# One order between pairs widened: xh and xl ahead of the next sine and of the next pair's planes, in every pair from batch 1 on

## The chip, the cores and the metric

The kernel runs on one core of one Trainium2 chip. The metric is the device time of one execution in microseconds, the median of several runs.

## What is computed

The reference is an attention over 8 batches of 8 heads (512 local rows with a window of 32 to each side, and 32 global rows that see all and are seen by all), followed by a layer with a cosine on all 8 x 544 rows. Cut to what matters:

```python
k_all = concat([k_g, k_l]); v_all = concat([v_g, v_l])
out_g = sm(scale * q_g @ k_all.T) @ v_all                       # 32 rows
s_ll  = where(abs(i - j) <= 32, scale * q_l @ k_l.T, -1e9)      # 512 rows
out_l = sm(concat([scale * q_l @ k_g.T, s_ll])) @ v_all
x = concat([out_g, out_l]) -> rows of 8 heads x 64 = 512
h = x @ w_in                # 512 -> 2048
out = (h * cos(h)) @ w_out  # 2048 -> 512
```

## The kernel before

**Attention** goes by batch b (0 to 7) and pair of heads p (0 to 3). For each of four windows i of 128 rows, TensorE makes the scores (`sc_a`, L527), VectorE adds the mask and takes the row minimum mn (`sc_b`, L545), ScalarE takes the exponential (`sc_c`, through `table_act`, L425), and VectorE the reciprocal of the sums (L564 and L565). Then `sc_d` makes two fp16 planes of the probabilities, the high one on ScalarE (L592) and what it misses on VectorE (L593): eight instructions a pair on each engine, all in the four buffers named planes. SP's queue transposes them (`sc_e`, L612) into pt, and TensorE multiplies pt by the values' two parts vh and vl into the PSUM tile acc (`av_a`, L645). `av_b` takes acc out of PSUM, again as two parts: **xh** on ScalarE (L665) and **xl** on VectorE (L666). xl is the last to read acc. The global rows have a path of their own, from gps (L681) to planes_g and gacc.

**Values.** The next batch's values are loaded into vr (`load_v`, one buffer, 1.25 MB), VectorE takes their maximum vm in one instruction (L481), TensorE spreads it over the partitions into pm_v (L459), VectorE makes the scale of it (L491), and `v_d` makes vh on ScalarE (L511) and vl on VectorE (L512), a pair at a time. The load of the next batch has to wait for the last vl.

**The layer** goes by chunks c of 256 rows, two to a batch (c = 2b and 2b + 1, which follow in the next batch's time), with eight steps j each, and one chunk at the end for the global rows. A step is 24 matmuls with xh and xl into the PSUM tile ph (L800); u on ScalarE (L822) and VectorE (L823), which brings h to its period; the sine w on ScalarE (`m1_c`, L425); its square on GpSimd (L838); gf on VectorE (L840); gh on ScalarE (L844); gl on GpSimd (L845); and, three steps later, 12 matmuls into po (L859 to L861). VectorE and ScalarE scale po into the output rows o.

**PSUM** has a pool of three buffers with the tag att, which ps, gps, acc, gacc and pm_v take in turn, three for ph and two for po.

**What sets the order.** Each piece of work is put at a slot and a phase by `at(slot, phase, ...)`; there are eight slots to a chunk. In batches 2 to 7 pair p of batch b has its time t = 16(b - 1) + 3 + 4p: scores at t - 7 and t - 5, exponentials at t - 4, planes at t - 3, transposes at t - 1, product, xh and xl at t. So the planes of the next pair (t + 4 - 3) come one slot behind xh and xl. From this listing a scheduler with a model of the engines' times makes each engine's final order, and it may let one instruction pass another where nothing forbids it. What forbids it are dependences on data and edges of the kind `order`, which the kernel adds with `tc.add_manual_dep`; such an edge fixes the order of two instructions of one engine, and puts no semaphore into the program. `table_act` has one that keeps exponentials and sines in the order in which they are written. A sine and an exponential use different function tables on ScalarE, so each change between them is an ACT_TABLE_LOAD (58 in the program).

Two such edges concern xh and xl. `av_b` keeps the two instructions of the batch's latest pair in `st["last_x", b]`. Where p is 0 and b over 1, `sc_d` puts the planes of the pair behind xh and xl of the batch before (that is, of its pair 3). And `m1_c` puts the sine of an odd chunk's last step behind xh of the pair 3 that stands there.

Of the kernel before, what the change touches and what calls it, by code (L numbers as in the profile page):

```python
# [57 lines left out]
NS = NJ // 2  # L58
# [60 lines left out]
def body(tc, qf, v, wi, wo, mask, out):  # L119
# [5 lines left out]
    with ExitStack() as ctx:  # L125
# [37 lines left out]
        def behind(ins, what, why="scale_first"):  # L163
            if st.get(what) is not None:
                tc.add_manual_dep(ins, st[what].name, order, reason=why)
# [253 lines left out]
        st = {}  # L419
        order = mybir.DependencyInfo(mybir.DependencyClass.NoSync, mybir.DependencyReason.DATA)  # L420
        last_act = {"Exp": None, "Sin": None}

        def table_act(kind, *a, **k):

            ins = nc.scalar.activation(*a, **k).ins  # L425
            for prev in last_act.values():
                if prev is not None:
                    tc.add_manual_dep(ins, prev.name, order, reason="act_table_group")
            last_act[kind] = ins
            return ins  # L430
# [131 lines left out]
        def sc_r(b, p):  # L562
            rr = st["sm", b, p]
            nc.vector.tensor_scalar(rr, rr, 1e-9, 2.0**-10, op0=ALU.add, op1=ALU.mult)  # L564
            nc.vector.reciprocal(rr, rr)  # L565

        def sc_d(b, p, i):
            if i == 0:
                sc_r(b, p)
            t, rr = st.pop(("t", b, p, i))[0], st["sm", b, p]  # L570
            w = WIN[i][1]
            pl = PLS[p][i] if b == 0 else (PL0, PL1, PL)[min(b, 2)]
            if pl in (3, 4):
                if pl == 3:
                    r = rr[:, 2 * i : 2 * i + 2]
                    rb = bass.AP(tensor=r.tensor, offset=r.offset, ap=[r.ap[0], (1, 2), (0, w)])
                    for h in range(2):
                        nc.gpsimd.tensor_tensor(t[:, h], t[:, h], rb[:, h], op=ALU.mult)
                if pl == 4:
                    for h in range(2):  # L580
                        nc.scalar.activation(t[:, h], t[:, h], AF.Copy, scale=rr[:, 2 * i + h : 2 * i + h + 1])
                hi = planes[i][:, :, 0, OFF[i] : OFF[i] + w]
                lo = planes[i][:, :, 1, OFF[i] : OFF[i] + w]
                nc.scalar.copy(hi, t)
                for h in range(2):
                    nc.gpsimd.tensor_tensor(lo[:, h], t[:, h], hi[:, h], op=ALU.subtract)
            else:
                for h in range(2):
                    hi = planes[i][:, h, 0, OFF[i] : OFF[i] + w]
                    lo = planes[i][:, h, 1, OFF[i] : OFF[i] + w]  # L590
                    r = rr[:, 2 * i + h : 2 * i + h + 1]
                    a = nc.scalar.activation(hi, t[:, h], AF.Identity, scale=r)  # L592
                    d = nc.vector.scalar_tensor_tensor(lo, t[:, h], r, hi, op0=ALU.mult, op1=ALU.subtract)  # L593
                    if (b, p) == (0, 3):
                        behind(d.ins, "dx")
                    if b > 1 and p == 0:
                        for ins, x in zip((a, d), st["last_x", b - 1]):
                            tc.add_manual_dep(ins.ins, x.name, order, reason="products_first")

        def sc_e(b, p, i):  # L600
# [55 lines left out]
        def av_b(b, p):  # L656
            if p == 0:
                st["x", b] = (
                    ap_.tile([P, NPAIR, SL], F16, tag="xh", name=f"xh_{b}"),
                    ap_.tile([P, NPAIR, SL], F16, tag="xl", name=f"xl_{b}"),  # L660
                )
            xh, xl = st["x", b]
            acc = st.pop(("acc", b, p))
            sx = xs[:, p : p + 1]
            hi = nc.scalar.activation(xh[:, p], acc, AF.Identity, scale=sx)  # L665
            lo = nc.vector.scalar_tensor_tensor(  # L666
                xl[:, p], acc, sx, xh[:, p], op0=ALU.mult, op1=ALU.subtract
            )
            st["last_x", b] = (hi.ins, lo.ins)


        GW = ((SG, 288), (SG + 288, 256))
# [153 lines left out]
        def m1_c(c, j):  # L826
            u, w = st["u", c, j]
            ins = table_act("Sin", w, u, AF.Sin, scale=st["cs", c][0])
            x = st.get(("last_x", (c + 1) // 2))
            if c % 2 and j == NS - 1 and x is not None:  # L830
                tc.add_manual_dep(ins, x[0].name, order, reason="products_first")

        def m1_d(c, j):
            w = st.pop(("u", c, j))[1]
# [67 lines left out]
        def attn_rest(b, p, o):  # L902
            for i in range(4):
                at(o["sc"][i], PA, sc_a, b, p, i)
                at(o["sc"][i], PA if o["tight"] else PC, sc_b, b, p, i)
                at(o["ex"], PI, sc_c, b, p, i)
                at(o["sd"], PF, sc_d, b, p, i)
                at(o["tr"][i], PA2, sc_e, b, p, i)
            at(o["vd"], PF2, v_d, b, p)
            at(o["av"], PA, av_a, b, p)  # L910
            at(o["av"] if b else -6, PF, av_b, b, p)
            if p % 2:
                g = p // 2
                for k in range(2):
                    at(o["gs"][k], PA, g_a, b, g, k)
                    at(o["gs"][k], PA if o["tight"] else PC, g_b, b, g, k)
                at(o["ex"], PI, g_c, b, g)
                at(o["gd"], PF2, g_d, b, g)
                at(o["ge"], PA2, g_e, b, g)
                at(o["gf"] if b else GF0, PG, g_f, b, g)  # L920
                at(o["gf"] if b else GF0, PH2, g_g, b, g)
# [64 lines left out]
        for c in range(NC + 1):  # L986
            at(NS * c, -11, chunk_scales, c)
            for j in range(NS):
                s = NS * c + j
                if c == 0 and j < JS:  # L990
                    for kc in range(NPAIR):
                        at(-5 + kc, PJ, m1_a, c, j, kc)
                else:
                    at(s, ma, m1_a, c, j)
                at(s, mb, m1_b, c, j)
                at(s + 1, mc, m1_c, c, j)
                at(s + 1, md, m1_d, c, j)
                at(s + lag, m2, m2_a, c, j)
            for k in range(CT // P):
                at(NS * c + NS - 1 + lag, ob, m2_b, c, k)  # L1000
                at(NS * c + NS + lag, oc, m2_c, c, k)
# [82 lines left out]
```

## Time and profile before

| | us |
|---|---|
| median of 3 runs (977.45 to 977.69) | 977.54 |
| the profiled execution | 977.96 |
| its span, first to last instruction | 976.2 |
| busy in the span: TensorE matmuls | 911.0 |
| ScalarE | 669.3 |
| VectorE | 572.2 |
| GpSimd | 398.6 |

All times below are of the profiled execution, from the start of its span. The mean clock granted to TensorE was 0.962 of full speed. Batch 0's attention and the loading of the weights fill the first 100 us; batch 1's attention runs beside the first layer steps until about 205 us; then batches 2 to 7 follow each other at 106 us each, every one beside the layer of the batch before it; from about 835 us on there is the layer alone. A wait is the idle time of an engine ahead of an instruction, with what ended it named behind the arrow.

### The profile page before, as it was taken

The page shows a single profiled execution, that of the slowest core. Times are in us where ns is not written, and L with a number is a line of the kernel's source. Part 1 is how long each engine was busy: PE and PEld are TensorE (multiplying, and loading weights), DVE is VectorE, ACT ScalarE, POOL GpSimd, SP SyncE. Part 2 cuts the span into 40 slices and gives each one's busy share as a digit, 9 for nine tenths or more (in the row PEclk, how much of TensorE's full clock was granted, in tenths as well). Part 3 has the DMA queues.
Part 4 walks back from the last instruction along what each step waited for, and adds up shares of the span by engine and source line. Part 5 has one row for each costly group of instructions (what it writes and reads, how often), then busy time and mean ns, then how long its engine had stood idle before and what let it go on. Part 6 is the DMA issues. An engine that isn't in the chain of part 4 may idle for free. (4 is left out here: it accounts for less than half of the span.)

```text
span 976.2 us, 20500 instructions
## 1 busy us (share of the span) xinstructions
PE 911.0 (93%) x7963; PEld 605.2 (62%) x7963; DVE 572.2 (59%) x1544; ACT 669.3 (69%) x1435; POOL 398.6 (41%) x412
## 2 busy tenths in 40 slices
PE   6657988899999999999999999999999999999996
PEld 4446655556666565666566666666566666666663
DVE  5997979846465655566565746565656554423221
ACT  6896899857677676766777677757677776433441
POOL 5856654433324243433333332434343434344441
PEclk7667999999999999999999999999999999999998
DMA  9935158535333442545252632354252433000000
GB/s 370 379 113 194 44 149 182 136 98 95 80 76 74 133 84 59 109 120 109 45 130 44 158 71 62 78 137 83 66 108 66 83 66 57 23 1 22 1 24 21
DMA packets 155178, 96.44 MB, mean 99 GB/s; under 512 B 141000, under 2 KB 141128, under 8 KB 153288
## 3 DMA queue, kind: packets, MB, share of 16 engines
q1 hardware_dynamic: 155080, 95.13, 38.7%
q8 instruction: 62, 1.02, 0.4%
q14 instruction: 36, 0.29, 0.1%
HBM read 51.59 MB, written 8.91 MB: 62 GB/s over the span
## 5 line engine op out<-in xcount | busy, mean ns | idle before, releaser
L800 PE MATMUL ph<-xh,wi_h 128*128 128x256 f16 x1024 | 282.9, 276 | 1.3 <-DVE gf L840 1.1
L800 PE MATMUL ph<-xl,wi_h 128*128 128x256 f16 x1024 | 282.0, 276 | 0.0
L800 PE MATMUL ph<-xh,wi_l 128*128 128x256 f16 x1024 | 281.9, 275 | 0.0
L838 POOL TENSOR_TENSOR w<-w 128x512 f32<-128x512 f32 x136 | 143.6, 1056 | 294.1 <-ACT w L425 294.1
L845 POOL TENSOR_TENSOR gl<-gf,gh 128x512 f16<-128x512 f32 x136 | 161.5, 1188 | 221.8 <-ACT gh L844 221.7
L800 PEld LDWEIGHTS <-wi_h 128*128 128x128 f16 x2176 | 207.1, 99 | 66.9 <-issue 27.6
L860 PE MATMUL po<-wo_hl,gh 128*128 128x512 f16 x544 | 206.3, 379 | 0.9 <-POOL wo_hl L213 0.9
L859 PE MATMUL po<-wo_hl,gh 128*128 128x512 f16 x544 | 204.3, 379 | 2.5 <-ACT wo_hl L239 1.9
L861 PE MATMUL po<-wo_hl,gl 128*128 128x512 f16 x544 | 205.9, 379 | 0.3 <-POOL gl L845 0.3
L844 ACT CAST gh<-gf 128x512 f16<-128x512 f32 x136 | 83.2, 613 | 128.7 <-DVE gf L840 128.7
L840 DVE SCALAR_TENSOR_TENSOR gf<-w,ph 128x512 f32<-128x512 f32 x136 | 93.1, 684 | 127.2 <-POOL w L838 126.1
L823 DVE SCALAR_TENSOR_TENSOR u<-u,cm,ph 128x512 f32<-128x512 f32 x136 | 101.2, 745 | 103.3 <-ACT u L822 103.3
L425 ACT ACTIVATE w<-u,ca 128x512 f32<-128x512 f32 x136 | 98.0, 721 | 88.8 <-DVE u L823 87.9
L425 ACT ACTIVATE t<-t,mn 128x192 f32<-128x192 f32 (+1 forms) x256 | 116.7, 457 | 18.5 <-DVE mn L545 18.1
L800 PEld LDWEIGHTS <-wi_l 128*128 128x128 f16 x1088 | 107.6, 99 | 14.2 <-issue 0.5
L822 ACT ACTIVATE u<-ph,cm 128x512 f32<-128x512 f32 x136 | 92.0, 678 | 23.9 <-PE ph L800 23.9
L593 DVE SCALAR_TENSOR_TENSOR planes<-t,sm,planes 128x192 f16<-128x192 f32 (+1 forms) x232 | 96.1, 475 | 3.6 <-ACT planes L592 2.9
L861 PEld LDWEIGHTS <-gl 128*128 128x128 f16 x544 | 53.2, 98 | 64.0 <-issue 1.2
L545 DVE CUSTOM_DVE_ANT_0 t<-ps,msk 128x192 f32<-128x192 f32 (+1 forms) x256 | 84.0, 366 | 13.6 <-PE ps L527 10.5
L592 ACT ACTIVATE planes<-t,sm 128x192 f16<-128x192 f32 (+1 forms) x232 | 86.3, 454 | 2.1 <-ACT t L425 2.1
L859 PEld LDWEIGHTS <-gh 128*128 128x128 f16 x544 | 52.6, 98 | 52.5 <-issue 3.1
L860 PEld LDWEIGHTS <-gh 128*128 128x128 f16 x544 | 53.2, 98 | 50.8 <-issue 1.8
(149 smaller groups left out, 1095.3 us busy)
## 6 DMA issues: line engine op xcount, KB each, us to landing
qkr<-qf SPq DMA_DIRECT2D x31, 608.0 KB, 4.5
vr<-v SPq DMA_DIRECT2D x8, 1280.0 KB, 6.3
out<-o SPq DMA_DIRECT2D x34, 256.0 KB, 2.1
raw_wi<-wi SPq DMA_DIRECT2D x6, 1024.0 KB, 13.4
wo_hl<-wo SPq DMA_DIRECT2D x8, 512.0 KB, 11.4
raw_wm<-wo SPq DMA_DIRECT2D x8, 512.0 KB, 5.7
raw_wo<-wo SPq DMA_DIRECT2D x8, 512.0 KB, 4.2
raw_wi<-wi SPq DMA_DIRECT2D x4, 512.0 KB, 12.2
```

The lines of the kernel that those rows point to most:

```text
L425: ins = nc.scalar.activation(*a, **k).ins
L592: a = nc.scalar.activation(hi, t[:, h], AF.Identity, scale=r)
L593: d = nc.vector.scalar_tensor_tensor(lo, t[:, h], r, hi, op0=ALU.mult, op1=ALU.subtract)
L800: nc.tensor.matmul(ph[:, a], w[:, kc, f], x[:, kc, q], start=first and ip == 0, stop=last and ip == 2, skip_group_check=True,)
L822: nc.scalar.activation(u, ph, AF.Identity, bias=m)
L823: nc.vector.scalar_tensor_tensor(u, u, m, ph, op0=ALU.subtract, op1=ALU.subtract)
L838: nc.gpsimd.tensor_tensor(w, w, w, op=ALU.mult)
L840: nc.vector.scalar_tensor_tensor(gf, w, 0.5, st.pop(("ph", c, j)).rearrange("p a b -> p (a b)"), op0=ALU.subtract, op1=ALU.mult,)
L845: nc.gpsimd.tensor_tensor(gl, gf, gh, op=ALU.subtract)
L859: nc.tensor.matmul(po[k], gh[:, q], wo_h[:, f], start=(f == 0), stop=False)
L860: nc.tensor.matmul(po[k], gh[:, q], wo_l[:, f], start=False, stop=False)
L861: nc.tensor.matmul(po[k], gl[:, q], wo_h[:, f], start=False, stop=(f == NJ - 1))
```

## The change

The two edges are to hold for every pair. `st["last_x"]` is kept by batch and pair. In `sc_d`, from batch 2 on, the planes of every pair (not of pair 0 alone) come behind xh and xl of the pair before: on ScalarE behind xh, on VectorE behind xl. `av_b` also leaves xh in `st["new_x"]`, and the next sine that `m1_c` writes takes it out and is put behind it, from chunk 1 on (not an odd chunk's last sine alone). No operation is added or taken away.

```diff
-                    if b > 1 and p == 0:
-                        for ins, x in zip((a, d), st["last_x", b - 1]):
+                    if b > 1:
+                        for ins, x in zip((a, d), st["last_x", *((b, p - 1) if p else (b - 1, 3))]):
                             tc.add_manual_dep(ins.ins, x.name, order, reason="products_first")
@@ av_b
-            st["last_x", b] = (hi.ins, lo.ins)
+            st["last_x", b, p] = (hi.ins, lo.ins)
+            st["new_x"] = hi.ins
@@ m1_c
-            x = st.get(("last_x", (c + 1) // 2))
-            if c % 2 and j == NS - 1 and x is not None:
-                tc.add_manual_dep(ins, x[0].name, order, reason="products_first")
+            x = st.pop("new_x", None)
+            if c and x is not None:
+                tc.add_manual_dep(ins, x.name, order, reason="products_first")
```

From the function `m1_c` on, the changed kernel's lines are one further down (the sine's square is L839 there, gh L845), and so from `av_b` on for what follows it. In the rows, xh_b and acc_b_p carry batch and pair, t_b_p_i also the window, u, w, ph, gf and gh chunk and step; planes0 to planes3 are the four windows' planes. The number at a name's end only tells buffers apart.

The first place is ScalarE at pair 1 of batch 3, with the planes of pair 2 and the layer's steps 4.7 and 5.0. Before:

```order
L822 ACTIVATE u_4_7_4713<-ph_4_7_4688,cm_4_4079 128x512
L592 ACTIVATE planes0_76<-t_3_2_0_4529,sm_3_2_4774 128x192 x2
L592 ACTIVATE planes1_78<-t_3_2_1_4533,sm_3_2_4774 128x224 x2
L592 ACTIVATE planes2_80<-t_3_2_2_4673,sm_3_2_4774 128x224 x2
L592 ACTIVATE planes3_82<-t_3_2_2_4673,sm_3_2_4774 128x192 x2
L425 ACT_TABLE_LOAD
L425 ACTIVATE w_4_7_4714<-u_4_7_4713,ca_4_4078 128x512
L665 ACTIVATE xh_3_4455<-acc_3_1_4731,xs_90 128x512
L844 CAST gh_4_7_4784<-gf_4_7_4787 128x512
L822 ACTIVATE u_5_0_4816<-ph_5_0_4791,cm_4_4079 128x512
L425 ACTIVATE w_5_0_4817<-u_5_0_4816,ca_4_4078 128x512
```

And in the changed kernel:

```order
L823 ACTIVATE u_4_7_4713<-ph_4_7_4688,cm_4_4079 128x512
L665 ACTIVATE xh_3_4455<-acc_3_1_4731,xs_90 128x512
L425 ACT_TABLE_LOAD
L425 ACTIVATE w_4_7_4714<-u_4_7_4713,ca_4_4078 128x512
L592 ACTIVATE planes0_76<-t_3_2_0_4529,sm_3_2_4774 128x192 x2
L592 ACTIVATE planes1_78<-t_3_2_1_4533,sm_3_2_4774 128x224 x2
L592 ACTIVATE planes2_80<-t_3_2_2_4673,sm_3_2_4774 128x224 x2
L592 ACTIVATE planes3_82<-t_3_2_2_4673,sm_3_2_4774 128x192 x2
L823 ACTIVATE u_5_0_4816<-ph_5_0_4791,cm_4_4079 128x512
L845 CAST gh_4_7_4784<-gf_4_7_4787 128x512
L425 ACTIVATE w_5_0_4817<-u_5_0_4816,ca_4_4078 128x512
```

xh moves from the place behind the planes, the table load and the sine to the place ahead of all three; the table load and the sine move ahead of the planes, and u of the next step ahead of gh. The other steady batches read alike. At pairs 0 and 2 only the planes come to stand behind xh.

The second place is VectorE there. Before:

```order
L823 SCALAR_TENSOR_TENSOR u_4_7_4713<-u_4_7_4713,cm_4_4079,ph_4_7_4688 128x512
L593 SCALAR_TENSOR_TENSOR planes0_76<-t_3_2_0_4529,sm_3_2_4774,planes0_76 128x192 x2
L593 SCALAR_TENSOR_TENSOR planes1_78<-t_3_2_1_4533,sm_3_2_4774,planes1_78 128x224 x2
L593 SCALAR_TENSOR_TENSOR planes2_80<-t_3_2_2_4673,sm_3_2_4774,planes2_80 128x224 x2
L593 SCALAR_TENSOR_TENSOR planes3_82<-t_3_2_2_4673,sm_3_2_4774,planes3_82 128x192 x2
L666 SCALAR_TENSOR_TENSOR xl_3_4456<-acc_3_1_4731,xs_90,xh_3_4455 128x512
L840 SCALAR_TENSOR_TENSOR gf_4_7_4787<-w_4_7_4714,ph_4_7_4688 128x512
L823 SCALAR_TENSOR_TENSOR u_5_0_4816<-u_5_0_4816,cm_4_4079,ph_5_0_4791 128x512
```

And in the changed kernel:

```order
L824 SCALAR_TENSOR_TENSOR u_4_7_4713<-u_4_7_4713,cm_4_4079,ph_4_7_4688 128x512
L666 SCALAR_TENSOR_TENSOR xl_3_4456<-acc_3_1_4731,xs_90,xh_3_4455 128x512
L593 SCALAR_TENSOR_TENSOR planes0_76<-t_3_2_0_4529,sm_3_2_4774,planes0_76 128x192 x2
L593 SCALAR_TENSOR_TENSOR planes1_78<-t_3_2_1_4533,sm_3_2_4774,planes1_78 128x224
L841 SCALAR_TENSOR_TENSOR gf_4_7_4787<-w_4_7_4714,ph_4_7_4688 128x512
L593 SCALAR_TENSOR_TENSOR planes1_78<-t_3_2_1_4533,sm_3_2_4774,planes1_78 128x224
L593 SCALAR_TENSOR_TENSOR planes2_80<-t_3_2_2_4673,sm_3_2_4774,planes2_80 128x224 x2
L593 SCALAR_TENSOR_TENSOR planes3_82<-t_3_2_2_4673,sm_3_2_4774,planes3_82 128x192 x2
L824 SCALAR_TENSOR_TENSOR u_5_0_4816<-u_5_0_4816,cm_4_4079,ph_5_0_4791 128x512
```

xl moves ahead of the eight planes, and gf among them. TensorE's own order is the same before and after in batches 2 to 7. On SP's queue two query loads move ahead of the next pair's transposes.

The third place is ScalarE in batch 1, around the product of pair 2 (planes of pair 3, step 1.5 of the layer). Before:

```order
L425 ACTIVATE w_1_5_2421<-u_1_5_2420,ca_0_1248 128x512
L227 ACTIVATE z_wo15_1854<-raw_wo15_1852,wsc_109 128x512
L592 ACTIVATE planes0_76<-t_1_3_0_2200,sm_1_3_2376 128x192 x2
L592 ACTIVATE planes1_78<-t_1_3_1_2204,sm_1_3_2376 128x224 x2
L592 ACTIVATE planes2_80<-t_1_3_2_2214,sm_1_3_2376 128x224 x2
L592 ACTIVATE planes3_82<-t_1_3_3_2218,sm_1_3_2376 128x192 x2
L713 ACTIVATE planes_g_84<-gt_1_1_2079,gsm_1_1_2385 128x544
L844 CAST gh_1_2_2107<-gf_1_2_2110 128x512
L511 ACTIVATE vh_2_1_2656<-vr_2_1717,vs_2_1863 128x640
L511 ACTIVATE vh_2_2_3050<-vr_2_1717,vs_2_1863 128x640
L239 CAST wo_hl_88<-z_wo15_1854 128x512
L665 ACTIVATE xh_1_1993<-acc_1_2_2436,xs_90 128x512
```

And in the changed kernel:

```order
L592 ACTIVATE planes0_76<-t_1_3_0_2200,sm_1_3_2376 128x192 x2
L592 ACTIVATE planes1_78<-t_1_3_1_2204,sm_1_3_2376 128x224 x2
L592 ACTIVATE planes2_80<-t_1_3_2_2214,sm_1_3_2376 128x224 x2
L592 ACTIVATE planes3_82<-t_1_3_3_2218,sm_1_3_2376 128x192 x2
L511 ACTIVATE vh_2_2_3050<-vr_2_1717,vs_2_1863 128x640
L823 ACTIVATE u_1_5_2420<-ph_1_5_2395,cm_0_1249 128x512
L845 CAST gh_1_2_2107<-gf_1_2_2110 128x512
L714 ACTIVATE planes_g_84<-gt_1_1_2079,gsm_1_1_2385 128x544
L665 ACTIVATE xh_1_1993<-acc_1_2_2436,xs_90 128x512
L239 CAST wo_hl_88<-z_wo15_1854 128x512
L823 ACTIVATE u_1_6_2532<-ph_1_6_2507,cm_0_1249 128x512
L425 ACTIVATE w_1_5_2421<-u_1_5_2420,ca_0_1248 128x512
```

The sine of step 1.5 moves from ahead of the planes of pair 3 to behind xh of pair 2. In the same way the sine of step 1.1 now stands behind xh of pair 0, and that of step 1.3 behind xh of pair 1; between 120 and 200 us the order of all engines differs.

## Rows read from the trace of the kernel before

**Rows 1.** Busy time of two stretches: length, engines with counts, clock, DMA share, GB/s

```profile
150.00:200.00 50.00, 44.10 (x416) 27.47 (x414) 41.16 (x107) 47.15 (x110) 21.47 (x23) 1.00 0.67 146
700.00:800.00 100.00, 100.00 (x928) 67.05 (x928) 57.77 (x168) 72.50 (x163) 37.73 (x34) 1.00 0.39 79
```

**Rows 2.** Waits of TensorE from 205 us to the end: total, times, longest

```profile
PE pm_v L459 <- DVE xl L666: 9.9, 5, 2.3
PE gps L681 <- DVE mn L545: 2.2, 3, 1.8
```

**Rows 3.** Timeline of ScalarE, pair 1 of batch 3: start, duration, instruction, [idle before]

```profile
361.88 0.66 ACT L822 ACTIVATE u<-ph,cm 128x512 f32<-128x512 f32 x1
362.50 2.98 ACT L592 ACTIVATE planes<-t,sm 128x192 f16<-128x192 f32 x8
365.49 1.28 ACT L425 ACT_TABLE_LOAD   x1
366.79 0.72 ACT L425 ACTIVATE w<-u,ca 128x512 f32<-128x512 f32 x1
367.42 0.67 ACT L665 ACTIVATE xh<-acc,xs 128x512 f16<-128x512 f32 x1
369.50 0.62 ACT L844 CAST gh<-gf 128x512 f16<-128x512 f32 x1 [1.41 <-DVE gf L840]
370.02 0.68 ACT L822 ACTIVATE u<-ph,cm 128x512 f32<-128x512 f32 x1
...
374.17 0.62 ACT L844 CAST gh<-gf 128x512 f16<-128x512 f32 x1 [1.87 <-DVE gf L840]
```

**Rows 4.** Timeline of VectorE, the same place

```profile
363.24 2.85 DVE L593 SCALAR_TENSOR_TENSOR planes<-t,sm,planes 128x192 f16<-128x192 f32 x8
368.12 0.75 DVE L666 SCALAR_TENSOR_TENSOR xl<-acc,xs,xh 128x512 f16<-128x512 f32 x1 [2.03 <-ACT xh L665]
```

**Rows 5.** Timeline of TensorE, pair 1 of batches 3, 5 and 6

```profile
360.18 0.22 PE L645 MATMUL acc<-pt,vl 128*64 128x128 f16 x2
...
581.38 0.26 PE L459 MATMUL pm_v<-d_v,ones 128*128 128x128 bf16 x1 [2.28 <-DVE xl L666]
581.45 0.42 PE L800 MATMUL ph<-xh,wi_h 128*128 128x256 f16 x1
...
687.76 0.27 PE L800 MATMUL ph<-xh,wi_h 128*128 128x256 f16 x1
```

**Rows 6.** Busy time of 8 us around pair 1 of batches 3 and 6

```profile
366.00:374.00 8.00, 5.70 (x37) 4.00 (x34) 3.32 (x9) 4.00 (x6) 3.23 (x3) 0.79 0.59 111
685.00:693.00 8.00, 5.69 (x43) 3.60 (x39) 3.45 (x9) 3.83 (x7) 3.23 (x3) 1.00 0.55 106
```

**Rows 7.** Timeline of VectorE and TensorE, pair 0 of batches 3 and 4

```profile
332.04 2.82 DVE L481 TENSOR_REDUCE vm<-vr 128x1 f32<-128x2560 f32 x1 [4.37 <-DMA vr<-v]
335.50 0.64 PE L681 MATMUL gps<-qkr 128*32 128x256 f32 x8 [1.80 <-DVE mn L545]
441.85 0.64 PE L681 MATMUL gps<-qkr 128*32 128x256 f32 x8 [0.15 <-DVE mn L545]
```

**Rows 8.** Timeline of GpSimd and VectorE, batch 1

```profile
180.32 1.49 POOL L838 TENSOR_TENSOR w<-w 128x512 f32<-128x512 f32 x1
181.03 4.34 DVE L593 SCALAR_TENSOR_TENSOR planes<-t,sm,planes 128x192 f16<-128x192 f32 x8
```

**Rows 9.** Timeline of ScalarE, batch 1

```profile
150.36 0.71 ACT L425 ACTIVATE w<-u,ca 128x512 f32<-128x512 f32 x1
154.27 0.66 ACT L665 ACTIVATE xh<-acc,xs 128x512 f16<-128x512 f32 x1
178.34 0.72 ACT L425 ACTIVATE w<-u,ca 128x512 f32<-128x512 f32 x1
185.60 0.69 ACT L665 ACTIVATE xh<-acc,xs 128x512 f16<-128x512 f32 x1
```

**Rows 10.** Waits of all engines over the whole span

```profile
ACT xh L665 <- PE acc L645: 4.4, 4, 2.2
```

## The prediction

> **What bounds the kernel now.** I read four views. First the stretches: between 700 and 800 us TensorE is busy all of the time at full clock, while VectorE and ScalarE are busy 58 and 73 of 100 us [rows 1]. From about 205 us on TensorE is therefore the bound, and what it loses there is lost to the kernel. Second, its waits from 205 us on: 9.9 us in five waits of pm_v for the low plane xl (L459 for L666, the longest 2.3 us), and 2.2 us in three waits of gps (L681) for a row minimum [rows 2]. The five waits stand once in each of batches 2 to 6, at pair 1; the first is a short one (0.7 us, what is left of 9.9 beside four of 2.3), and batch 7 has no next values, so no pm_v. Third, the timelines around pair 1 of batch 3. TensorE ended acc at 360.4 us [rows 5], but ScalarE took xh only at 367.42: after the last u came eight planes of pair 2 (2.98 us), a table load (1.28) and a sine (0.72) [rows 3]. xl followed at 368.12 [rows 4], 7.7 us after the product was ready. xl is what frees acc's PSUM buffer, and pm_v takes it. Fourth, the clock, next.
>
> **What such a wait costs.** The idle time itself, and in three of the five places the clock. After the wait before 581.38 the next matmuls took 0.42 us each; after the equally long one before 687.76 one took 0.27 us [rows 5]. The mean granted clock of the 8 us around the first kind is 0.79 (batches 3, 4 and 5 read alike), around the second 1.00 [rows 6]. That is a stretch at 1.2 GHz instead of 2.4 GHz: 8 x 0.21 = 1.7 us of full-speed work lost, three times, 5.0 us.
>
> **The change, part by part.** No operation is added or removed; ScalarE has as many table loads as before, and the edges are orders on one engine, without semaphores of their own. What moves is xh on ScalarE and xl on VectorE.
>
> *Pair 1 of batches 2 to 6.* xh now stands right behind the last u. In batch 3 that u ends at 362.54, and acc has been over for 2.1 us, so xh runs to 363.2 and xl to about 364.0 (0.67 and 0.75 us long). TensorE wants pm_v some 2.3 us before 368.92, that is at 366.6: 2.6 us of slack. The wait goes: **9.9 us**. With it goes what dropped the clock: **5.0 us**.
>
> *Pair 0 of batch 3.* Here gps waited 1.80 us for a minimum that stood on VectorE behind the maximum vm over the next values (2.82 us), which itself waited 4.37 us for their load [rows 7]. The load is released by the last vl of the batch, at the end of a chain over ScalarE, VectorE and GpSimd that began at the pair 1 before. ScalarE gets on earlier there, so I count these **1.8 us** as gained too; this is the less certain term.
>
> *What is given back.* The same chain runs in batches 4 to 6, and there it was just in time: in batch 4 gps waited 0.15 us [rows 7]. It was in time because TensorE had lost 2.3 + 1.7 = 4.0 us at the pair 1 before. Without that loss ScalarE must come earlier by 4.0 us as well. How much does it? The sine moves ahead of the planes: xh, load and sine end at 362.54 + 0.67 + 1.28 + 0.72 = 365.2, not at 367.5: 2.3 us. Then come the planes, to 368.2, and the next u, which stood at 370.02 [rows 3], since the cast in front of it waited 1.41 us for gf. So u gains 1.8 us at least; and the changed order puts the two casts that waited 1.41 and 1.87 us [rows 3] behind other work, so up to the whole 4.0 us can be won on the way to pair 0. Between ends of 0 and 2.2 us given back in each of three batches I take 0.8, nearer the low end, because the idle time ahead of casts and sines lies in the stretch between. Batch 3 followed a wait of only 0.7 us, so I take 0.3 there. Together **2.7 us back**.
>
> One thing speaks for more. GpSimd's square follows the sine, so it now falls beside VectorE's planes. In batch 3 the eight planes took 2.85 us alone [rows 4]; at 181.03 eight of them took 4.34 us beside a square of 1.49 us and another GpSimd operation [rows 8]. That is up to 1.5 us, and it is inside my 0.8, which is why this is not 0. The Trainium skill has the rule for it: SBUF — State Buffer, section "SBUF: two separate sides", says that VectorE operations with two SBUF inputs and GpSimd operations that read SBUF hold one port pair in turn, each for its whole instruction. The trace agrees (2.85 against 4.34 us). By that rule alone the planes would lose about the square of 180.32, 1.49 us, and the next u would gain 0.3 instead of 1.8 us, which speaks for the late maximum below.
>
> *Pairs 0 and 2.* xh fills time in which ScalarE waits for the reciprocal ahead of the planes; xl puts VectorE's planes back by its 0.75 us at most. The transposes that follow are wanted a pair later, some 20 us on. Cost 0; if the cover were gone, 0.75 us a pair.
>
> *SP.* Two query loads move ahead of the transposes of the next pair, since the planes come later. The queue waits for planes anyway. Cost 0.
>
> *Batch 1, 120 to 200 us.* Here all orders move. ScalarE has the same work without a pause, so its end should not. The sine of step 5 moves from 178.34 to behind xh of pair 2, which ran at 185.60 to 186.3: 7.9 us later [rows 9]. If nothing covered that it would cost 7.9 us; its cover is the out-projection of the steps before, which TensorE still has to do. The other end: TensorE was idle 5.9 us between 150 and 200 us [rows 1], and some of it could go, since acc of pair 1 stands earlier. Between +7.9 and -5.9 I take **0**.
>
> **Sum.** 9.9 + 5.0 + 1.8 - 2.7 = 14.0 us. The profiled execution took 977.96 us (span 976.2 and 1.8 around it), 0.42 above the median of 977.54; from the median the forecast is **963.5 us**.
>
> **The rivals.**
> - *The late maximum moves in.* The chain to vm takes its full time, as in batch 3, and gps waits 1.8 us in each of batches 3 to 6: 7.2 us back instead of 2.7, **968.0**. For it: batch 3 is the one batch that had nearly no wait at pair 1 before it, and it is the one with the 1.8; and the port above. Against it: the sine is 2.3 us earlier. Chance 0.20.
> - *The clock falls all the same*, somewhere else in batches 3 to 5: 5.0 us less, **968.5**. For it: the wait of 2.3 us in batch 6 was not followed by a fall, so the wait alone does not decide. Against it: from 205 us on no fall stands anywhere but behind these waits. Chance 0.08.
> - *Batch 1 gains*, by half of its idle time, and less is given back: **959**. Chance 0.06.
> - *The sine waits for the product* (slower). ScalarE now may not start a sine before xh, and xh needs acc from TensorE. In four places xh already waits for acc, 4.4 us in all, 1.1 each [rows 10]. If each of the 21 newly ordered pairs (0 to 2 of batches 1 to 7) stood as long, and TensorE then for its PSUM buffers, that is 23.1 us: 977.5 - 14.0 + 23.1 = **986.6**. It decides from 14.0 / 21 = 0.67 us a pair on. Against it: at pair 1 acc was over 2.1 us before its new turn, and in batch 1 xh of pair 0 ran 3.9 us after the sine that it now precedes [rows 9]. Chance 0.06.
> - *Nothing comes of it*: batch 1 takes what the others give (its 7.9 us, and the late maximum's 4.5 more). About **976**. Chance 0.04.
>
> **How the numbers follow.** The forecast itself has 0.56. Its own range is 960 to 967. The range for 8 in 10 takes in the first three rivals: its low end is the forecast without anything given back and with half of batch 1's idle time, 963.5 - 2.7 - 3.0 = 957.8, so 957.5; its high end is the late maximum with 2 us lost in batch 1, 970. A measurement of this kernel tells a difference from none at about 0.2%, 2 us. Faster than 975.6: 0.56 + 0.20 + 0.08 + 0.06 = 0.90; slower than 979.5: 0.06; within: 0.04.
>
> **What would show it.** Right: TensorE's list of waits from 205 us on has no pm_v for xl; xh of pair 1 starts within 1 us of the last u; the granted clock is 1.00 from 205 us to the tail. The given-back term shows as gps waiting for mn in batches 4 to 6, under 1 us each. Wrong would be gps waits of 1.8 us and more (the late maximum), sines or xh waiting for acc in the waits of ScalarE (the slower case), stretches at half clock without a wait in front (the clock), or more idle time of TensorE between 120 and 205 us than before (batch 1).

## The result and the profile after

The changed kernel takes **959.97 us** (median of 5 runs, 959.23 to 962.02), the kernel before 977.54 us beside it: a ratio of 0.9818, interval 0.9802 to 0.9834, or 17.6 us less. The forecast was 963.5 us, its own range 960 to 967, the wider one 957.5 to 970.

From the page of the changed kernel, its span and the engines' busy time:

```profile
span 957.5 us, 20487 instructions
...
PE 909.4 (95%) x7963; PEld 604.0 (63%) x7963; DVE 569.3 (59%) x1544; ACT 668.4 (70%) x1435; POOL 399.7 (42%) x412
```

Over the whole span every engine is busy about as long as it was (TensorE 909.4 against 911.0 us), and what shrank is TensorE's idle time, from 65.2 to 48.1 us. That sum hides the clock. From batch 2's first product to the end of batch 7's last, TensorE's idle time fell from 12.1 to 1.5 us and its busy time from 590.3 to 585.3, since three stretches at half clock are gone; in batch 1 the changed kernel has such a stretch that the kernel before has not, 6.8 us long at 136 us. TensorE's waits from 205 us on, which answer to [rows 2], are now one row (total us, times, longest):

```profile
PE gps L682 <- DVE mn L545: 1.4, 3, 0.7
```

pm_v for xl is gone from the list. The timeline of ScalarE at pair 1 of batch 3, against [rows 3] (start, duration, instruction, and the idle time before it):

```profile
355.85 0.67 ACT L823 ACTIVATE u<-ph,cm 128x512 f32<-128x512 f32 x1
356.42 0.67 ACT L665 ACTIVATE xh<-acc,xs 128x512 f16<-128x512 f32 x1
357.38 1.28 ACT L425 ACT_TABLE_LOAD   x1 [0.29 <-DVE u L824]
358.68 0.72 ACT L425 ACTIVATE w<-u,ca 128x512 f32<-128x512 f32 x1
359.31 2.97 ACT L592 ACTIVATE planes<-t,sm 128x192 f16<-128x192 f32 x8
362.18 0.67 ACT L823 ACTIVATE u<-ph,cm 128x512 f32<-128x512 f32 x1
362.75 0.60 ACT L845 CAST gh<-gf 128x512 f16<-128x512 f32 x1
```

VectorE, TensorE and GpSimd (the sine's square) there, against [rows 4] and [rows 5]:

```profile
357.22 0.75 DVE L666 SCALAR_TENSOR_TENSOR xl<-acc,xs,xh 128x512 f16<-128x512 f32 x1
359.78 1.64 DVE L593 SCALAR_TENSOR_TENSOR planes<-t,sm,planes 128x192 f16<-128x192 f32 x3 [1.81 <-ACT planes L592]
361.35 0.68 DVE L841 SCALAR_TENSOR_TENSOR gf<-w,ph 128x512 f32<-128x512 f32 x1
361.94 1.83 DVE L593 SCALAR_TENSOR_TENSOR planes<-t,sm,planes 128x224 f16<-128x224 f32 x5
```

```profile
361.07 0.23 PE L459 MATMUL pm_v<-d_v,ones 128*128 128x128 bf16 x1
```

```profile
359.48 1.04 POOL L839 TENSOR_TENSOR w<-w 128x512 f32<-128x512 f32 x1 [3.65 <-ACT w L425]
```

xh starts where the last u ends, xl is done at 357.97, and pm_v takes the buffer at 361.07 without a wait, 3.1 us later. The stretch of 8 us around it (busy time by engine, then the granted clock), against [rows 6]:

```profile
355.00:363.00 8.00, 8.00 (x63) 5.67 (x62) 5.01 (x11) 7.70 (x19) 1.87 (x2) 1.00 0.09 18
```

TensorE is busy all of it and at full clock, 1.00 where it was 0.79.

Where the 18.7 us between the two spans (976.2 and 957.5) went can be read place by place. The last product matmul (L645) of each pair starts at a time that both traces have; the difference after minus before, and its step from place to place:

| up to the product of | after - before | step | what lies between |
|---|---|---|---|
| batch 0 | -1.43 | -1.43 | same order in both kernels |
| batch 2, pair 0 | -3.03 | -1.60 | batch 1 |
| batch 2, pair 2 | -3.77 | -0.74 | pm_v at pair 1 |
| batch 3, pair 1 | -5.48 | -1.70 | gps at pair 0 |
| batch 3, pair 2 | -9.50 | -4.02 | pm_v and half clock |
| batch 4, pair 1 | -9.23 | +0.27 | gps |
| batch 4, pair 2 | -13.25 | -4.02 | pm_v and half clock |
| batch 5, pair 1 | -12.92 | +0.33 | gps |
| batch 5, pair 2 | -16.80 | -3.88 | pm_v and half clock |
| batch 6, pair 1 | -16.36 | +0.44 | gps |
| batch 6, pair 2 | -18.72 | -2.36 | pm_v |
| end | -18.73 | 0.0 | |

From batch 2 on that is 15.7 us. Each kernel has one profiled execution, and the table and the rest below are read from it. The first row is no effect of the change: up to there all engines have the same instructions in the same order, and in the other kernels below, which share them too, the same place lies between 0.07 us later and 1.6 us earlier than in the kernel before.

### The profile page after: what moved, and what is told of

The parts are those of the page before. It is cut to its first block, busy times and chain, and to the rows that moved or that the text cites. A ratio compares the mean times of both kernels' runs of the same rounds, so it can differ in the third digit from the quotient of the medians.

```text
span 957.5 us, 20487 instructions
## 1 busy us (share of the span) xinstructions
PE 909.4 (95%) x7963; PEld 604.0 (63%) x7963; DVE 569.3 (59%) x1544; ACT 668.4 (70%) x1435; POOL 399.7 (42%) x412
## 4 chain that ended last, share of the span: by engine, by line
PE 51%; ACT 15%; DVE 11%; issue 9%; POOL 8%; DMA 5%; SPq 0%; ACTq 0%; POOLq 0%; DVEq 0%
PE ph L801 21%; PE po L861 8%; PE po L862 8%; PE po L860 8%; ACT t L425 4%; DMA vr<-v 3%; POOL w L839 3%; PE ps L527 3%; POOL gl L846 2%; ACT planes L592 2%; PE acc L645 2%; DVE gf L841 2%; ACT gh L845 2%; ACT L425 2%; POOL wi_l L213 2%
## 5 line engine op out<-in xcount | busy, mean ns | idle before, releaser
L839 POOL TENSOR_TENSOR w<-w 128x512 f32<-128x512 f32 x136 | 143.6, 1056 | 259.1 <-ACT w L425 241.2
L845 ACT CAST gh<-gf 128x512 f16<-128x512 f32 x136 | 83.4, 615 | 112.8 <-DVE gf L841 112.7
```

The source lines that it names most:

```text
L839: nc.gpsimd.tensor_tensor(w, w, w, op=ALU.mult)
L845: nc.scalar.copy(gh, gf)
```

## The experiments

In what follows "the rest" is the time from batch 2's first product to the end, read as in the table: 745.6 us before, 729.9 after (15.7 less). Ratios are against the kernel before on the same chip, whose median there was between 978.6 and 979.1 us.

### One edge without the other

```diff
 planes_edge_alone: m1_c as before
-            x = st.pop("new_x", None)
-            if c and x is not None:
+            x = st.get(("last_x", (c + 1) // 2, 3))
+            if c % 2 and j == NS - 1 and x is not None:
 sine_edge_alone: sc_d as before
-                    if b > 1:
+                    if b > 1 and p == 0:
```

> Only the edge in sc_d is widened (planes of every pair behind xh and xl of the pair before); the sine's edge stays as in the kernel before. At pair 1 xh now stands behind the last u, the table load and the sine, and xl behind gf. Theory (xl frees the PSUM buffer that pm_v takes): xh starts 1.28 + 0.72 us after u ends, xl ends about 0.5 us after TensorE wants pm_v, so four waits of pm_v of 0.3 to 0.8 us stay, no stretch at half clock follows them, batch 1 is as before: 977.5 - (9.9 - 2.2) - 5.0 - 1.8 + 1.0 = 964. Rival (the planes' place doesn't matter, the sine's does): waits of 2.3 us stay and the time is 976 to 978.

> Only the edge in m1_c is widened (each sine after a product behind its xh, from chunk 1 on); planes as in the kernel before. At pair 1 xh stands behind the eight planes but ahead of table load and sine. Theory: xl ends some 2.0 us earlier than before, so four waits of pm_v of 0.2 to 0.7 us stay, without half clock behind them; batch 1 has the changed order. 977.5 - (9.9 - 1.8) - 5.0 - 1.8 + 1.0 - 1.6 = 962. Rival (only both edges together help): above 970.

Measured: 974.14 us (ratio 0.9949, 0.9933 to 0.9966) and 972.59 us (0.9932, 0.9917 to 0.9947). TensorE's waits from 205 us on, first with the planes' edge alone, then with the sine's:

```profile
PE gps L682 <- DVE mn L545: 9.7, 4, 2.8
PE pm_v L459 <- DVE xl L666: 3.2, 4, 0.8
```

```profile
PE gps L682 <- DVE mn L545: 6.6, 4, 2.0
PE gacc L737 <- DVE mn L545: 2.5, 2, 1.2
PE pm_v L459 <- DVE xl L666: 0.6, 2, 0.3
```

The waits of pm_v came out as expected (0.8 and 0.3 us). But the time did not: what they had given was lost again at gps, 9.7 and 6.6 us, in waits of up to 2.8 us. Both expectations were 10 us too low, and for the same reason: I had taken the 1.0 us of gps waits in the full change for granted. The time of the sine's edge alone is the one that its rival named (above 970), though not for the rival's reason: one edge does take most of the waits of pm_v away, and only with both does gps not wait instead.

### Which pairs and which batches

```diff
 from_batch_2
+            if b > 1 or p == 3:
                 st["new_x"] = hi.ins
 pair_1_alone
-                    if b > 1:
+                    if b > 1 and p % 2 == 0:
+            if p == 3 or (b > 1 and p == 1):
                 st["new_x"] = hi.ins
 pairs_1_and_2
-                    if b > 1:
+                    if b > 1 and p != 1:
+            if p == 3 or (b > 1 and p in (1, 2)):
                 st["new_x"] = hi.ins
 all_but_pair_1
-                    if b > 1:
+                    if b > 1 and p != 2:
+            if b <= 1 or p != 1:
                 st["new_x"] = hi.ins
 batch_1_alone (sc_d as before)
+            if b <= 1 or p == 3:
                 st["new_x"] = hi.ins
```

> The change in batches 2 to 7 alone; batch 1 keeps the order of the kernel before on TensorE, GpSimd and nearly so on the others. Theory: the steady batches give 15.7 us (the ledger of the two traces: 0.7 at pair 1 of batch 2, 1.7 at pair 0 of batch 3, 4.0, 4.0, 3.9 and 2.4 at pair 1 of batches 3 to 6, and 1.0 back at pair 0 of batches 4 to 6): 961.8. Rival (batch 1 gives as much as the traces show up to its end, 3.0): 963.

> The change at pair 1 of batches 2 to 7 alone (planes of pair 2 and the next sine behind xh and xl of pair 1); all else as in the kernel before. Theory: pairs 0 and 2 cost and give nothing, so the same as from batch 2: 961.8, within 1 us of it, and no wait of pm_v. Rival (xl ahead of the planes at pairs 0 and 2 costs up to 0.75 us a pair): 953 to 957, below it by up to 9 us.

> The change everywhere except at pair 1 of batches 2 to 7. Theory: the five waits of pm_v stay (9.9 us) and so do the stretches at half clock; only batch 1 gives something, 1.6 us: 976. Rival (the order of the sines at pairs 0 and 2 helps): under 972.

> The change in batch 1 alone. Theory: TensorE's idle time between 148 and 205 us falls from 6.8 to about 2.2 us, and the end of batch 1 comes 1.6 us earlier; the steady batches are as before, with waits of 2.3 us for pm_v: 976. Rival (nothing from batch 1, the forecast's own term): 977.5. Rival (the late sine of step 1.5 costs): 979 and more.

> The change at pairs 1 and 2 of batches 2 to 7, not at pair 0. Theory (each xh put into ScalarE's pause ahead of the planes saves its own 0.6 us on the way to the last vl, and gps returns it): gps waits of about 0.5 + 0.55 = 1.0 us in batches 4 to 6, the last vl ends 8.9 us before the product of pair 0 does (9.5 with all pairs, 8.3 with pair 1 alone), 963. Rival (one of the two pairs gives all): 961 or 965.

| kernel | median, us | ratio (interval) | the rest, against before | waits of gps, pm_v |
|---|---|---|---|---|
| from_batch_2 | 961.08 | 0.9817 (0.9804 to 0.9830) | -16.1 | 1.2, 0 |
| pairs_1_and_2 | 963.58 | 0.9845 (0.9832 to 0.9859) | -14.3 | 3.0, 0 |
| pair_1_alone | 965.46 | 0.9863 (0.9848 to 0.9878) | -11.7 | 4.9, 0 |
| all_but_pair_1 | 970.80 | 0.9922 (0.9908 to 0.9937) | -5.2 | 4.8, 7.0 |
| batch_1_alone | 975.08 | 0.9968 (0.9957 to 0.9979) | -0.3 | 7.4, 4.4 |

The batches from 2 on give all that can be told from the ratios (0.9817 against 0.9818). Pair 1 alone gives 4.4 us less than all pairs: pairs 0 and 2, which the forecast put down at nothing, matter, each by about half, and the expectation of pair_1_alone (961.8) missed. Without pair 1 the kernel still gains, which I had not expected (970.8 instead of 976, below the 972 of the rival). Its waits of pm_v are 1.73 to 1.75 us instead of 2.3, which fits the 0.55 us that the next traces show for pair 0, and no half clock follows them.

In batch_1_alone the order from 213 us on is that of the kernel before, and batches 2 to 7 take as long (-0.3), but the loss stands elsewhere. Behind its wait of pm_v in batch 3, 2.31 us, the clock did not fall. From batch 4 on TensorE then waits 1.9 to 2.2 us at gps, with half clock behind, and only 0.6 to 0.8 at pm_v. What one place gave, the next took.

How pairs 0 and 2 gain is seen in the traces of pair_1_alone and from_batch_2, since TensorE stands at the same time in both (the product of batch 3, pair 1 within 0.02 us). Two of ScalarE's waits from 205 us on stand in the kernel before and in pair_1_alone with the same numbers, and neither stands in from_batch_2 (total, times, longest; the lines of the kernel before):

```profile
ACT gt L425 <- DVE gmn L694: 3.9, 8, 0.5
ACT planes L592 <- ACT t L425: 2.1, 4, 0.5
```

The second one is ScalarE's pause ahead of the planes, and it stands at pair 0 of batches 3 to 6 alone. The first one is the exponential of the global rows, gt, waiting for their minimum gmn; it stands at pair 2 of every batch, and at pair 0 of batches 2 and 7. ScalarE and VectorE at pair 2 of batch 3, in pair_1_alone:

```profile
383.22 0.66 ACT L824 ACTIVATE u<-ph,cm 128x512 f32<-128x512 f32 x1
383.84 2.98 ACT L592 ACTIVATE planes<-t,sm 128x192 f16<-128x192 f32 x8
386.73 0.67 ACT L665 ACTIVATE xh<-acc,xs 128x512 f16<-128x512 f32 x1
387.87 0.75 ACT L425 ACTIVATE gt<-gt,gmn 128x544 f32<-128x544 f32 x1 [0.48 <-DVE gmn L696]
...
384.58 2.85 DVE L593 SCALAR_TENSOR_TENSOR planes<-t,sm,planes 128x192 f16<-128x192 f32 x8
387.35 0.48 DVE L696 CUSTOM_DVE_ANT_0 gt<-gps,zero,gmn 128x256 f32<-128x256 f32 x1
```

and in from_batch_2:

```profile
382.67 0.67 ACT L824 ACTIVATE u<-ph,cm 128x512 f32<-128x512 f32 x1
383.24 0.67 ACT L665 ACTIVATE xh<-acc,xs 128x512 f16<-128x512 f32 x1
383.81 2.97 ACT L592 ACTIVATE planes<-t,sm 128x192 f16<-128x192 f32 x8
386.68 0.74 ACT L425 ACTIVATE gt<-gt,gmn 128x544 f32<-128x544 f32 x1
...
384.04 0.48 DVE L696 CUSTOM_DVE_ANT_0 gt<-gps,zero,gmn 128x256 f32<-128x256 f32 x1
385.11 2.85 DVE L593 SCALAR_TENSOR_TENSOR planes<-t,sm,planes 128x192 f16<-128x192 f32 x8
```

u is 0.55 us earlier, which is what pair 0 won: there xh fills the pause of 0.53 us ahead of the planes. At pair 2 ScalarE has no such pause, for in pair_1_alone the planes follow u at once; xh ahead of them or behind them is the same to ScalarE. What goes there is the wait of 0.48 us for gmn. On VectorE gmn stood behind the eight planes, and with xl it has moved ahead of them. gt's exponential so comes 1.19 us earlier, 0.55 from pair 0 and the rest, some 0.64, from pair 2. The sines, the planes and the values' parts that follow on ScalarE keep those 1.19 us for 36 us, down to the last vl, the load of the next values that it releases, and the maximum vm. VectorE and TensorE in batch 4, in pair_1_alone:

```profile
424.34 0.88 DVE L512 SCALAR_TENSOR_TENSOR vl<-vr,vs,vh 128x640 f16<-128x640 f32 x1
431.78 2.82 DVE L481 TENSOR_REDUCE vm<-vr 128x1 f32<-128x2560 f32 x1 [4.55 <-DMA vr<-v]
435.24 0.64 PE L683 MATMUL gps<-qkr 128*32 128x256 f32 x8 [1.68 <-DVE mn L545]
```

and in from_batch_2:

```profile
423.17 0.88 DVE L512 SCALAR_TENSOR_TENSOR vl<-vr,vs,vh 128x640 f16<-128x640 f32 x1
430.58 2.82 DVE L481 TENSOR_REDUCE vm<-vr 128x1 f32<-128x2560 f32 x1 [3.41 <-DMA vr<-v]
434.04 0.64 PE L683 MATMUL gps<-qkr 128*32 128x256 f32 x8 [0.46 <-DVE mn L545]
```

1.17 us at vl, 1.20 at vm, 1.20 at gps. With vm ahead of the minima, the wait of gps in batches 4 to 6 follows how far ahead of the end of pair 0's product the last vl ends: 9.5 us ahead with all pairs (waits of 0.26 to 0.68), 9.0 with pairs 1 and 2 (0.94 to 1.07), 8.3 with pair 1 alone (1.5 to 1.8), 7.4 with the planes' edge alone (2.5 to 2.8). From the end of vl it takes 6.1 to 6.8 us to vm, then 2.8 us for vm itself.

### Is it the idle time that costs the clock?

```diff
 fill_the_wait: the kernel before, in spread_b
+            if int(name[1:]) > 3:
+                po = st["po", 2 * int(name[1:]) - 4]
+                for k in range(NFILL):    # 10
+                    fill = nc.tensor.matmul(po[k % 2], zero[:, :P].bitcast(F16), wo_h[:, k],
+                                            start=False, stop=False, skip_group_check=True)
             mm = nc.tensor.matmul(pm, ones13, st.pop(("diag", name)), start=True, stop=True)
+                tc.add_manual_dep(mm.ins, fill.ins.name, order, reason="fill_first")
```

> The kernel before, with ten matmuls by a tile of zeros (512 columns, added to the running po, so nothing changes) on TensorE ahead of pm_v at pair 1 of batches 3 to 6; every engine's order is else the same. They fill the wait of 2.3 us with 2.1 to 2.2 us of work. Theory (it is the idle time that drops the clock): the waits' time stays, xl is as late, but no stretch at half clock stands behind the places; 977.5 - 3 x 1.7 = 972.4. Rival (the clock falls there whatever TensorE does): 977.5. Rival (the zeros cost more than they cover): above 978.

Measured: 979.23 us, ratio 1.000 (0.999 to 1.001). The places themselves did what the theory says. TensorE at pair 1 of batch 3, and the 8 us around:

```profile
367.15 2.33 PE L464 MATMUL po<-wo_hl,zero 128*128 128x512 f16 x10
369.54 0.22 PE L468 MATMUL pm_v<-d_v,ones 128*128 128x128 bf16 x1
369.60 0.27 PE L811 MATMUL ph<-xh,wi_h 128*128 128x256 f16 x1
```

```profile
366.00:374.00 8.00, 7.95 (x54) 4.87 (x53) 3.38 (x10) 4.60 (x7) 3.21 (x3) 1.00 0.66 128
```

No half clock follows, neither here nor behind the three other filled waits, nor behind the four of fill_and_minima_first below; behind unfilled waits of the same length it fell three times of five. From the product of pair 1 to that of pair 2 it takes 1.65, 1.66 and 1.72 us less than before in batches 3, 4 and 5, and no less in batch 6, where the clock had not fallen. That is the forecast's 1.7 us, three times. But the kernel gained nothing, and the expected 972.4 was missed, since gps took it back (the same wait was 2.2 us in the kernel before [rows 2]):

```profile
PE gps L692 <- DVE mn L556: 8.1, 4, 3.5
```

In batch 4 this is the forecast's given-back term at its full size: TensorE comes 1.7 us earlier to pair 0, the chain to vm is where it was, and 1.8 us go back. In batch 5 it is 5.0 us, more than the filling had saved in one place: there vm started 8.05 us behind the end of the last vl, not 6.1 to 6.8, for a reason that the trace leaves open, gps waited 3.5 us, and half clock followed. On ScalarE one vh and one gh a batch changed places as well, from batch 3 on.

### The buffer that pm_v takes

```diff
 pm_v_other_buffer: the kernel before
-            early = name.startswith(("qk0", "v0"))
+            early = name.startswith(("qk0", "v0")) or (name[0] == "v" and int(name[1:]) > 2)
```

> The kernel before with every instruction in the same order on every engine; from batch 2 on pm_v takes a PSUM buffer of the tag ph instead of att, so it no longer waits for xl. Theory (the late xl costs only because pm_v takes its buffer): the waits of 2.3 us and the half clock behind them go though xh and xl stay as late as they were, 977.5 - 9.9 - 5.0 - 1.8 + 1.0 = 962 to 964, if the step that then lacks a ph buffer doesn't wait. Rival (the wait moves to the next user of a buffer, ph for gf or ps for xl): waits of 1 to 2.3 us under another name, 968 to 978.

Measured: 982.26 us, ratio 1.0030 (1.0014 to 1.0045): slower. The wait has another name and is longer:

```profile
PE ph L800 <- DVE gf L840: 12.4, 5, 2.8
```

VectorE at pair 1 of batch 3, and TensorE's step behind pm_v:

```profile
368.82 0.75 DVE L666 SCALAR_TENSOR_TENSOR xl<-acc,xs,xh 128x512 f16<-128x512 f32 x1 [2.02 <-ACT xh L665]
369.49 0.68 DVE L840 SCALAR_TENSOR_TENSOR gf<-w,ph 128x512 f32<-128x512 f32 x1
...
370.23 0.28 PE L800 MATMUL ph<-xh,wi_h 128*128 128x256 f16 x1 [2.75 <-DVE gf L840]
```

pm_v ran without a wait, but the step behind it then lacked a ph buffer until gf, and gf stands on VectorE behind the same late xl. So it isn't enough to free the one buffer: the step of the layer is as late as the product there. The rival was right that the wait moves, and the time is above its range: from batch 2 on this kernel loses 5.4 us more than the kernel before, with half clock behind four of the five waits instead of three.

### The order of the maximum

```diff
 minima_first (the same edit on pair_1_alone and on fill_the_wait for the two others)
+                    st["red", b, p, i] = nc.vector.tensor_tensor_reduce(   # in sc_b
+                mx = nc.vector.tensor_reduce(m, st["vr", b], ...)          # in v_a
+                r = st.get(("red", b - 1, 1, 3))
+                if b > 3 and r is not None:
+                    tc.add_manual_dep(mx.ins, r.ins.name, order, reason="minimum_first")
```

> The changed kernel with one more order on VectorE: from batch 3 on the maximum vm stands behind the row minima (L545) of pair 1's last windows, which it stood ahead of. Theory (what is given back is gps waiting for minima that stand behind vm, and vm for its load): the scores are ready some 3 us before vm's load is, so the minima run in VectorE's idle time, gps doesn't wait (1.4 us gone), vm is late by 0 to 1.5 us, which pm_v some 25 us later doesn't feel: 1.4 us below the changed kernel, 958.6. Rival (vm's delay pushes u and the chain of the layer's step behind it): a new wait of ph or gps of 1 us and more, 960 to 963.

> The change at pair 1 alone (965.46 us, gps waits of 1.5 to 1.8 us in batches 4 to 6) with the same order of vm behind the minima. Theory: the work of pairs 0 and 2 paid only by bringing the last vl, and so vm, 1.2 us earlier; with the minima ahead of vm that no longer matters, the 4.9 us of gps waits go and the time is that of minima_first within 1.5 us: 959 to 961. Rival (pairs 0 and 2 gain something else): 963 to 965.

> The kernel before with the ten zero matmuls in the wait of pm_v and vm behind the minima. Theory: filling the wait saved 1.7 us at each of three places and lost 8.1 us to gps behind vm; without that loss the gain stays: 977.5 - 5.0 - 1.8 = 971, no wait of gps over 0.3 us from 205 us on. Rival (the zeros cost what the clock gives): 975 to 978.

| kernel | median, us | ratio (interval) | the rest, against before | waits of gps |
|---|---|---|---|---|
| minima_first | 958.76 | 0.9796 (0.9783 to 0.9809) | -17.5 | none |
| pair_1_and_minima_first | 959.74 | 0.9810 (0.9796 to 0.9823) | -17.5 | none |
| fill_and_minima_first | 969.40 | 0.9905 (0.9891 to 0.9918) | -7.9 | none |

VectorE in batch 4 of minima_first, with the rows of minima on both sides of a gf:

```profile
426.90 0.38 DVE L548 CUSTOM_DVE_ANT_0 t<-ps,msk 128x224 f32<-128x224 f32 x1
...
428.67 0.09 DVE L548 DVE_READ_ACCUMULATOR2_ANT mn<- 128x1 f32 x1
430.24 2.82 DVE L481 TENSOR_REDUCE vm<-vr 128x1 f32<-128x2560 f32 x1 [1.49 <-DMA vr<-v]
```

The minima run in the time in which VectorE only waited for the load, vm starts 3.1 to 3.3 us ahead of the end of pair 0's product (2.8 to 3.4 in the changed kernel), and TensorE has no wait of over 0.1 us left from 205 us on. The two kernels with the change came out as expected, the third 1.6 us below its 971. pair_1_alone gains 5.8 us by it in the rest (11.7 to 17.5) and then equals the kernel with all pairs: what pairs 0 and 2 gave went only through vm and the minima. But the theory's reason, that a late vl no longer matters, was not put to the test, since the last vl is not late any more: it ends 9.6 us ahead of the end of pair 0's product, as in minima_first, and not 8.3. Minima that come ahead of vm also let ScalarE start the last of pair 1's exponentials earlier (it waited 4.1 us for them in batch 4 of pair_1_alone), and so its whole chain to the next vl. Filling the wait now pays 7.9 us in the rest, where its trace had lost 2.6, much of that at the late vm of batch 5. minima_first is the fastest kernel here; its median and the changed kernel's are 1.2 us apart with intervals that overlap, and the waits of gps that went are 1.4 us.

## Why the prediction was right, point by point

- **pm_v, 9.9 us, and the clock, 5.0 us.** Both were right. The steps at pair 1 in the first table add up to 15.0 us (0.74 + 4.02 + 4.02 + 3.88 + 2.36) against 14.9, the granted clock is 1.00 from 205 us up to the tail, and fill_the_wait measured the clock's part by itself.
- **Pair 0 of batch 3, 1.8 us.** Right: 1.70 us.
- **Given back, 2.7 us.** The mechanism was right, the size wrong: 1.0 us (0.27 + 0.33 + 0.44). The reason is the next step.
- **Pairs 0 and 2, cost 0.** This is the step that failed. I had asked what xh and xl push back there, and not what leaves ScalarE earlier. At pair 0 xh fills ScalarE's pause ahead of the planes, 0.55 us. At pair 2 the pause of which the forecast speaks is not there; some 0.64 us come from gmn, which moves ahead of VectorE's planes and which the forecast did not look at. Together they are worth 4.4 us between pair_1_alone and from_batch_2, 3.7 of them as shorter waits of gps in batches 4 to 6. Without them these waits would have been 1.5 to 1.8 us, near the 1.8 of the late maximum, my rival with 0.20, though not in batch 3, where that rival had one too; the time would have stood between the two (965.46, against 963.5 and 968.0). The forecast's 0.8 us a batch lay between the waits with and without pairs 0 and 2, so that its total came out near was in part luck: its account of where ScalarE gets earlier, by pair 1 alone, was wrong.
- **The shared port.** In the changed kernel the first three planes on VectorE took 1.64 us beside GpSimd's square, the last five 1.83 us, or 0.37 each, so the square costs some 0.5 us there. All of it is in the first plane, which began at 359.78, took 0.95 us instead of 0.41, and ended 0.21 us behind the square. In the rows of batch 1 in the kernel before [rows 8] it is the first and the last plane, 1.00 and 1.31 us, and each ended 0.22 us behind a GpSimd operation that had begun before it. The rule that the forecast drew on (the Trainium skill, SBUF — State Buffer, "SBUF: two separate sides") is that whichever starts first keeps the port pair for its whole instruction; the trace agrees. In the three cases the plane lost 0.54, 0.59 and 0.90 us, and 0.74, 0.78 and 1.09 us of GpSimd's operation were left when it began; the forecast had read the rule as the loss of the whole square, 1.49 us.
- **Batch 1, 0.** Not right in the trace: 1.6 us gained. From the end of batch 0's products to batch 2's first one, the five kernels with the new order in batch 1 take 147.1 to 148.3 us (the changed one 147.1), the nine with the old order 148.0 to 150.4. The medians don't settle it: batch_1_alone is 3.1 us below the kernel before (0.9968), minima_first 1.0 below pair_1_and_minima_first, which has the old order in batch 1 and the same rest, and between from_batch_2 and the changed kernel there is nothing (0.9817 and 0.9818). How much of it is in the 17.6 us stays open.
- **The slower rival.** Its mechanism exists, as the sign that the forecast named for it shows, and costs nothing: from 205 us on ScalarE waits for the product ahead of xh in eight places, 8.3 us, where it was three and 2.3, and TensorE waits for none of it.
- **The sum.** 963.5 forecast, 959.97 measured: 1.7 us less given back and, by the trace, 1.6 us gained in batch 1 make up 3.3 of the 3.5.

## What to carry to other kernels

A wait that is taken away lets the bound engine come earlier to its next meeting with the others, so look there first: here the next was some 70 us on, and in three experiments (one edge, the other edge, the filled wait) it took back from two thirds of what had been saved to more than all of it. Work on an engine that isn't the bound counts when its chain ends at such a meeting: an instruction put into that engine's own pause of 0.53 us was worth 0.55 there, and and one for which it waits, moved ahead of eight others on another engine, 0.64. And a long instruction that waits for a load should not stand in the queue ahead of short ones that the bound engine wants: one such order edge, on the kernel with pair 1 alone, was worth 5.7 us (965.46 to 959.74), where the other two pairs were worth 4.4.

## What the runs showed of the hardware

The fall of TensorE's clock to its lower level follows a wait, but not by the wait's length alone. Between 205 and 900 us the fourteen traces have 13 falls, each within a wait of 1.90 us or more or within 1.5 us of its end, and none at a wait of 1.82 us or less. Above that it goes both ways. Behind waits of gps of 1.90, 1.97 and 2.21 us it fell each time (batch_1_alone), behind waits of gps of 2.49, 2.63 and 2.77 us never (planes_edge_alone), though TensorE's order there is the same, and not behind 1.94 us in fill_the_wait; ahead of ph it fell at each of four waits of 2.72 to 2.75 us (pm_v_other_buffer); behind pm_v it fell after 2.28 to 2.31 us three times of five, and never after 1.73 to 1.75 us (all_but_pair_1). The stretches of 8 us behind the wait of 2.49 us and behind that of 1.90 us:

```profile
439.00:447.00 8.00, 8.00 (x66) 5.43 (x59) 7.12 (x24) 7.68 (x20) 1.16 (x1) 1.00 0.99 194
```

```profile
438.00:446.00 8.00, 8.00 (x50) 4.91 (x45) 6.74 (x23) 7.16 (x21) 1.16 (x1) 0.79 0.60 128
```

What decides between them is open. Early in the program it also varies without any change of order: between 135 and 145 us the granted clock was 1.00 in the kernel before, 0.83 in from_batch_2 and 0.62 in fill_the_wait, whose orders are the same until well behind that stretch, and 0.66 in the changed kernel.
